# Splitting late weight loads into 256 KB pieces and shifting TensorE's instruction stream by six tiny products

## The chip, the cores and the metric

The kernel runs on one core of a Trainium2 chip. The metric is the device time of one execution in microseconds (us). Before the change the median of three timed executions is 273.48 us (272.48 to 273.54). A further execution was profiled: it took 271.83 us, and the stretch between its first and last instruction, the span on which all times below are counted, is 270.0 us.

The engines are called by the profile's names: PE (matrix products), DVE (vector work), ACT (activations and copies), POOL (GpSimd, which here copies blocks and issues most loads) and SP (which issues the stores). PEld is the loading of PE's stationary operand.

## What is computed

Block-sparse attention over 4 batches, 8 heads, 768 positions and head size 64, followed by a two-layer network on the 3072 resulting rows of 512 numbers. Cut to what matters:

```python
scores = scale * np.matmul(q, k.transpose(0, 1, 3, 2))
mask = (np.abs(blk_i - blk_j) <= 1) | (blk_i == 0) | (blk_j == 0) | (blk_i == 23) | (blk_j == 23)
for qb in range(24):                       # blocks of 32 positions
    for kb in sampled_blocks[qb]:          # three sampled blocks for each
        mask[qb*32:(qb+1)*32, kb*32:(kb+1)*32] = True
attn = softmax(np.where(mask, scores, -1e9))
x = (attn @ v).transpose(0, 2, 1, 3).reshape(3072, 512)
h = x @ w_in                               # 512 x 2048
out = (0.5 * h * (1 + erf(h / sqrt(2)))) @ w_out   # 2048 x 512
```

## The kernel before, in words

The work is cut into eight units, two for each batch. A unit is 384 rows of the output: three quads of 128. The first unit of a batch also holds the two blocks that see every key (its "dense" rounds). For a unit the kernel runs attention, then `ffn1_step` eight times (products with `w_in`, Gelu on ACT, result in `g`), and the second layer (`ffn2_pieces`, products of `g` with `w_out`, 16 for a quad, m = 0 to 15) is not run by itself: its products are the filler that is strewn among the next unit's attention.

The order of all instructions is written out by hand. `attention` takes a plan, a string of words, and each engine executes its own instructions in the order in which the words issue them: `s7` is the scores of round 7 (PE), `m7` the maxima (DVE), `e7` the exponentials (ACT), `t7` the transposition (DVE), `wb` the products with the values for group b (PE), `db` the division (DVE), `ob` the turning of the result (PE and ACT), `f4` four products from the filler, `xb` an extra step of that letter, `G` the load of the Gelu table on ACT. An upper-case `O` splits the copy in two. Unit 0 has no second layer before it, so its filler is `idle_products`: products whose result nobody reads.

Unit 0 has rounds 0 to 3 (dense), 4 and 5 (group a), 6 and 7 (group b), 8 and 9 (group c); round 9 has one block row instead of two, so 8 products instead of 16. In its plan `xa`, `xb`, `xc` begin the first layer ahead of its step (`ffn1_ahead`, whose triples are m, i and the number of columns done).

Loads go through POOL's queue, in the order of the program, between POOL's own copies. `w_in` is loaded in four column quarters (`load_w_in`, 0 to 3, needed by `ffn1_step` from m = 0, 4, 8 and 12), `w_out` in two halves (`load_w_out`, m = 0 to 7 and 8 to 15). Quarters 2 and 3 and both halves are issued in `values_of(0)` and `values_of(2)`, the words `xv0` and `xv2`, among POOL's 33 copies of sampled value blocks (into `kn` and `g`, used as spare room). Then `later_keys` (word `xl`) issues the keys and queries of batch 1: kn heads 0 to 3, qn heads 0 to 3, kn heads 4 to 7, qn heads 4 to 7. In `PLANS[1]`, the plan of unit 1, the words `xk0d`, `xk1`, `xq1d`, `xq0`, `xk2` and so on turn these, two heads at a time.

The matching lines of the profile: L361 scores, L486 and L447 products with values, L518 turning, L541 first layer, L584 second layer, L594 idle products, L241 turning of keys and queries, L161, L166 and L117 the loads of w_in, w_out and keys or queries.

Of the kernel before, what the change touches and what calls it, by code (L numbers as in the profile page):

```python
# [20 lines left out]
def kernel(  # L21
# [10 lines left out]
    nc = tc.nc  # L32
    P = 128
    B, H, S, D = q.shape
    assert (B, H, S, D) == (4, 8, 768, 64)
    BL = 32
# [8 lines left out]
    KC = NPR * BL  # L45
    BW = KC + 2 * VS
# [69 lines left out]
    def load_kq(dst, src, hs, b=0):  # L116
        nc.gpsimd.dma_start(out=dst[0:PP, hs],  # L117
                            in_=src[b, hs].rearrange("h (p i) d -> p h (i d)", i=PI))
# [36 lines left out]
        for h in VORDER[at]:  # L155
            load_v(b, h)

    def load_w_in(part, n=4):
        w = D_FF // n
        cols = slice(w * part, w * part + w)  # L160
        nc.gpsimd.dma_start(  # L161
            out=w_in_sb[:, :, cols], in_=moe_w_in[:, cols].rearrange("(ki p) f -> p ki f", p=P))

    def load_w_out(part, n=4):
        w = KOUT // n
        nc.gpsimd.dma_start(  # L166
            out=w_out_sb[:, w * part:w * part + w, :],
            in_=moe_w_out[P * w * part:P * w * (part + 1)].rearrange("(ko p) f -> p ko f", p=P))
# [141 lines left out]
    def gather(unit, js, at, c0=0, c1=BW, engine=None):  # L310

        src = k0 if (unit.b, c1) == (0, KC) else kvs[unit.b % 2][:, :, c0:c1]
        for j in js:
            for r in range(NR):
                to = sampled_values(unit, j, r) if c0 == KC else sampled(unit.place[j], r)[:, c0:c1]
                (engine or nc.vector).tensor_copy(to[:, None, :], src[:, bass.ds(at[j][r], 1), :])  # L316
# [270 lines left out]
                    finished.append((n, quad, slice(0, D_MODEL), op))  # L587
                yield

    def idle_products(m):  # L590

        op = psO.tile([P, D_MODEL], F32, name="op", tag="op")
        for _ in range(m):
            nc.tensor.matmul(op, lhsT=identity, rhs=qT0[:, 0:2, 0:2, :], start=True, stop=True)  # L594
            yield

    def store_finished():
# [109 lines left out]
    def values_of(t):  # L707

        def ask():
            js = grps[t]  # L710
            gather(units[0], js[:3], others, KC, BW, nc.gpsimd)
            if t != 1:
                load_w_in(2 + t // 2)
            gather(units[0], js[3:], others, KC, BW, nc.gpsimd)
            if t == 2:
                load_w_out(0, 2)
                load_w_out(1, 2)
        return ask

    def later_keys():  # L720
        for hs in HALVES:
            load_kq(kn, k, hs, 1)
            load_kq(qn, q, hs, 1)
        others.update(block_numbers(J1[8:], POOL))

    def more_numbers(js):
        def load():
            for c in range(0, len(js), 6):
                known.update(block_numbers(js[c:c + 6], DVE))
        return load  # L730
    attention(units[0], idle_products(32),
# [3 lines left out]
              {"l": later_keys, "p2": partial(later_pair, 0), "p3": partial(later_pair, 1),  # L735
               "h": lambda: fixed(0, None, 0, (0,)), "i": lambda: fixed(0, None, 0, (1, 2)),
               "j": lambda: fixed(0, None, 1),
# [1 line left out]
               "f2": lambda: fixed(2, nc.scalar.copy, 0), "v0": values_of(0), "v1": values_of(1),  # L739
               "v2": values_of(2), "n": more_numbers(J1[:3]),  # L740
               "a": lambda: ffn1_ahead(0, (0, 0, P), (0, 1, P)),
               "b": lambda: ffn1_ahead(0, (0, 0, 2 * P)),
               "c": lambda: ffn1_ahead(0, (0, 1, 2 * P), (2, 0, 2 * P), (2, 1, 2 * P))})

    def next_keys(b):
        place_keys(b)
        spare_key(keys(b))

    PLANS = {
# [109 lines left out]
```

## Time and profile before

| | |
|---|---|
| median of three timed executions | 273.48 us |
| profiled execution | 271.83 us |
| its span | 270.0 us |
| PE busy | 248.2 us (92%) |
| ACT busy | 205.6 us (76%) |
| DVE busy | 201.7 us (75%) |
| POOL busy | 103.8 us (38%) |
| span of unit 0's attention on PE (scores to the last turning) | 12.7 to 37.6 us |
| unit 0's first layer on PE, to its end | 37.4 to 49.5 us |
| unit 1's attention with unit 0's second layer | 49.5 to 71.9 us |

A timeline row of the profile reads: start and length in us, engine, line, operation, tile written <- tiles read, shape, count, and in brackets the idle time of the engine before it with what ended it. "issue" there means that the engine waited for nothing that the profile shows. In the page's part on DMA queues, q0 holds what POOL issues and q8 and q14 carry packets of the kind "instruction". In a row on DMA issues the last number is the median time from issue to landing.

### The profile page before, as it was taken

The page shows a single profiled execution, that of the slowest core. Times are in us where ns is not written, and L with a number is a line of the kernel's source. Part 1 is how long each engine was busy: PE and PEld are TensorE (multiplying, and loading weights), DVE is VectorE, ACT ScalarE, POOL GpSimd, SP SyncE. Part 2 cuts the span into 40 slices and gives each one's busy share as a digit, 9 for nine tenths or more (in the row PEclk, how much of TensorE's full clock was granted, in tenths as well). Part 3 has the DMA queues.
Part 4 walks back from the last instruction along what each step waited for, and adds up shares of the span by engine and source line. Part 5 has one row for each costly group of instructions (what it writes and reads, how often), then busy time and mean ns, then how long its engine had stood idle before and what let it go on. Part 6 is the DMA issues. An engine that isn't in the chain of part 4 may idle for free.

```text
span 270.0 us, 11525 instructions
## 1 busy us (share of the span) xinstructions
PE 248.2 (92%) x4909; PEld 143.6 (53%) x4944; DVE 201.7 (75%) x472; ACT 205.6 (76%) x379; POOL 103.8 (38%) x212
## 2 busy tenths in 40 slices
PE   0899688999999999999999999999999999999994
PEld 0634365455664665545555565455645655465544
DVE  7599768599998988599988987696979892981000
ACT  8789655987869867898779965987889676994611
POOL 7798970725974000943970004900040250000000
PEclk9999999999999999999999999999999999999999
DMA  6999489979999116922997019911101110111012
GB/s 96 187 187 143 70 130 200 206 138 137 93 169 154 41 44 133 129 17 87 140 158 130 22 64 140 99 41 45 39 4 41 44 41 0 41 44 41 0 39 83
DMA packets 75910, 24.41 MB, mean 90 GB/s; under 512 B 65489, under 2 KB 72914, under 8 KB 75858
## 3 DMA queue, kind: packets, MB, share of 16 engines
q0 software_dynamic: 57440, 13.64, 54.0%
q1 hardware_dynamic: 18418, 10.03, 14.5%
q8 instruction: 39, 0.64, 1.0%
q14 instruction: 13, 0.11, 0.1%
HBM read 27.26 MB, written 6.29 MB: 124 GB/s over the span
## 4 chain that ended last, share of the span: by engine, by line
PE 77%; ACT 9%; DVE 5%; issue 4%; DMA 3%; POOL 1%; POOLq 0%; ACTq 0%
PE hp L541 31%; PE op L584 23%; PE av L486 8%; PE sc L361 6%; ACT pp L404 3%; DMA qn<-in_q_dram 3%; ACT pp L408 2%; PE tx L518 2%; PE op L613 2%; PE pt L241 2%; PE av L447 2%; DVE pT L421 1%; DVE nm L387 1%; PE av L613 1%; DVE xh L506 1%
## 5 line engine op out<-in xcount | busy, mean ns | idle before, releaser
L541 PE MATMUL hp<-xT,w_in_sb 128*128 128x384 bf16 (+2 forms) x536 | 85.1, 319 | 1.3 <-issue 1.3
L584 PE MATMUL op<-w_out_sb,g 128*128 128x512 bf16 x302 | 75.5, 380 | 3.4 <-issue 2.3
L404 ACT ACTIVATE pp<-sc,nm 128x256 bf16<-128x256 f32 x176 | 73.8, 544 | 5.5 <-DVE nm L387 5.2
L541 PEld LDWEIGHTS <-w_in_sb 128*128 128x128 bf16 x536 | 51.2, 98 | 34.5 <-issue 1.5
L563 ACT ACTIVATE g<-hp 128x768 bf16<-128x768 f32 x56 | 45.1, 808 | 24.3 <-PE hp L541 24.2
L387 DVE TENSOR_REDUCE nm<-sc 128x4 f32<-128x1024 f32 (+1 forms) x48 | 52.9, 1115 | 13.9 <-PE sc L361 13.8
L584 PEld LDWEIGHTS <-g 128*128 128x128 bf16 x336 | 29.1, 98 | 34.1 <-issue 6.7
L316 DVE COPY gb<-kv 128x392 bf16 x177 | 35.4, 278 | 0.0
L421 DVE STREAM_TRANSPOSE pT<-pp 128x512 f32<-128x512 f32 (+1 forms) x48 | 30.5, 650 | 2.9 <-ACT pp L404 2.9
L172 POOL COPY mark<-gb 1x1 bf16<-1x1 bf16 x6 | 1.1, 179 | 80.7 <-DVE gb L316 80.7
L316 POOL COPY gb<-kv 128x392 bf16 x54 | 26.3, 537 | 13.7 <-PE av L486 13.4
L486 PEld LDWEIGHTS <-pT 64*32 64x32 bf16 (+1 forms) x2400 | 25.2, 91 | 8.1 <-issue 2.8
L486 PE MATMUL av<-kv,pT 64*32 64x130 bf16 (+1 forms) x1344 | 27.3, 221 | 1.6 <-issue 0.7
L526 ACT COPY xT<-tx 128x512 bf16<-128x512 bf16 (+3 forms) x32 | 13.6, 451 | 14.3 <-PE tx L518 14.3
L148 POOL DMA_DIRECT2D kv<-in_v_dram x32 | 22.9, 729 | 2.3 <-issue 2.2
L361 PE MATMUL sc<-gb,qT 64*32 64x256 bf16 x704 | 17.9, 274 | 2.8 <-issue 1.8
L432 ACT ACT_TABLE_LOAD x15 | 19.2, 1283 | 0.3
L361 PEld LDWEIGHTS <-qT 64*32 64x32 bf16 x832 | 9.8, 90 | 17.9 <-issue 9.8
L506 DVE TENSOR_TENSOR xh<-av,rec 128x512 bf16<-128x512 f32 (+2 forms) x28 | 18.2, 652 | 1.0
L390 DVE TENSOR_REDUCE nm<-sc 128x1 f32<-128x768 f32 x16 | 14.8, 946 | 4.2 <-PE sc L361 4.2
L408 ACT ACTIVATE pp<-sc,nm 128x768 bf16<-128x768 f32 x16 | 17.2, 1109 | 1.0 <-DVE nm L390 0.9
L568 ACT COPY os<-op 128x512 f32<-128x512 f32 (+1 forms) x23 | 13.2, 574 | 5.8 <-PE op L613 4.3
(81 smaller groups left out, 250.8 us busy)
## 6 DMA issues: line engine op xcount, KB each, us to landing
out_dram<-os SPq DMA_DIRECT2D x23, 256.0 KB, 2.1
kv<-in_v_dram POOLq DMA_DIRECT2D x32, 96.0 KB, 3.6
w_in_sb<-in_moe_w_in_dram POOLq DMA_DIRECT2D x4, 512.0 KB, 7.7
w_out_sb<-in_moe_w_out_dram POOLq DMA_DIRECT2D x2, 1024.0 KB, 13.3
kn<-in_k_dram POOLq DMA_DIRECT2D x4, 384.0 KB, 11.3
qn<-in_q_dram POOLq DMA_DIRECT2D x4, 384.0 KB, 12.6
qn<-in_q_dram POOLq DMA_DIRECT2D x12, 128.0 KB, 5.3
kn<-in_k_dram POOLq DMA_DIRECT2D x12, 128.0 KB, 5.4
```

The source lines that it names most:

```text
L148: nc.gpsimd.dma_start(out=kvs[b % 2][32 * hh:32 * hh + 32, 0:NB, c0:c0 + D], in_=v[b, h].rearrange("(n p) d -> p n d", p=BL))
L316: (engine or nc.vector).tensor_copy(to[:, None, :], src[:, bass.ds(at[j][r], 1), :])
L361: nc.tensor.matmul(o, lhsT=qT[rows, j // 4, pr, BL * (j % 4):BL * (j % 4) + BL], rhs=rhs(rows, pr), start=True, stop=True)
L387: nc.vector.tensor_reduce(out=nm[:, 0:2 * n].rearrange("p (g j) -> p g j", g=2), in_=A4[:, :, 0:n, :], op=ALU.max, axis=AX.X, negate=True)
L404: nc.scalar.activation(at[:, x // n, x % n], A[:, a:a + 256].rearrange("p (e c k) -> p e c k", e=2, k=BL), AF.Exp, bias=nm[:, x:x + 1])
L408: nc.scalar.activation(pp[:, 0:S].rearrange("p (c k e) -> p c e k", e=2, k=BL), A[:, 0:S].rearrange("p (c e k) -> p c e k", e=2, k=BL), AF ...
L421: nc.vector.transpose(pt.rearrange("p g c x -> p (g c) x")[:, :, 64 * s:64 * (s + n)].bitcast(F32), pp[:, 0:512 * n].bitcast(F32).rearrang ...
L486: nc.tensor.matmul(av[32 * s:32 * (s + w), h, VS * G:VS * G + V2], lhsT=pv[rows, G, c % 4, BL * s:BL * (s + w), c // 4], rhs=src[rows], st ...
L506: nc.vector.tensor_tensor(xh[rows, :, 0:m * D].rearrange("p h (g x d) -> p h g x d", x=2, d=D), a[:, :, :, 0:2 * D].rearrange("p h g (x d) ...
L541: nc.tensor.matmul(hp[:, i, c0:c1], lhsT=w_in_sb[:, ki, (m + i) * P:(m + i + 1) * P], rhs=xTs[n % 2][:, ki, c0:c1], start=(ki == 0), stop= ...
L563: nc.scalar.activation(g[:, m:m + 2, 0:T], hp[:, :, 0:T], AF.Gelu)
L584: nc.tensor.matmul(op, lhsT=g[:, m, t * P:(t + 1) * P], rhs=w_out_sb[:, m, :], start=(m == 0), stop=(m == KOUT - 1))
```

## The change

Four things change; no arithmetic of the result does.

1. Loads. `load_w_in` gets a number of pieces, and quarter 3 comes in two pieces along the rows (256 KB each). `w_out` comes in eight pieces of two m each (256 KB each) instead of two halves. Pieces 0 to 5 stand where the halves stood; pieces 6 and 7 are issued in `later_keys` behind the first load of keys.
2. Quarter 2 of `w_in` (the third) is issued behind all twelve copies of its group instead of behind nine.
3. `idle_products` gets a set of places at which the product has 32 x 32 outputs instead of 128 x 512. There are six of these, and they come ahead of the six full ones before `s7`, the eighth scores of unit 0. Four full idle products are added ahead of `wb`, and two are taken out behind `Oc`.
4. `ffn1_ahead` no longer does columns 128 to 256 of m = 0 ahead (8 products of 128 columns); `ffn1_step` then does columns 128 to 384 in 8 products of 256 columns instead of 8 of 128. In `PLANS[1]` one second-layer product moves from before `xk0d` to behind it.

```diff
-    def load_w_in(part, n=4):
+    def load_w_in(part, n=4, pieces=1):
         w = D_FF // n
         cols = slice(w * part, w * part + w)
-        nc.gpsimd.dma_start(
-            out=w_in_sb[:, :, cols], in_=moe_w_in[:, cols].rearrange("(ki p) f -> p ki f", p=P))
+        for ki in range(0, KIN, KIN // pieces):
+            rows = slice(ki, ki + KIN // pieces)
+            nc.gpsimd.dma_start(
+                out=w_in_sb[:, rows, cols],
+                in_=moe_w_in[P * rows.start:P * rows.stop, cols].rearrange("(ki p) f -> p ki f", p=P))
...
-    def idle_products(m):
+    def idle_products(m, small):
         op = psO.tile([P, D_MODEL], F32, name="op", tag="op")
-        for _ in range(m):
-            nc.tensor.matmul(op, lhsT=identity, rhs=qT0[:, 0:2, 0:2, :], start=True, stop=True)
+        for n in range(m + len(small)):
+            if n in small:
+                nc.tensor.matmul(op[0:BL, 0:BL], lhsT=identity[:, 0:BL], rhs=qT0[:, 0, 0, 0:BL], start=True, stop=True)
+            else:
+                nc.tensor.matmul(op, lhsT=identity, rhs=qT0[:, 0:2, 0:2, :], start=True, stop=True)
             yield
...
-            gather(units[0], js[:3], others, KC, BW, nc.gpsimd)
+            gather(units[0], js, others, KC, BW, nc.gpsimd)
             if t != 1:
-                load_w_in(2 + t // 2)
-            gather(units[0], js[3:], others, KC, BW, nc.gpsimd)
+                load_w_in(2 + t // 2, pieces=1 + t // 2)
             if t == 2:
-                load_w_out(0, 2)
-                load_w_out(1, 2)
+                for part in range(6):
+                    load_w_out(part, 8)
...
             load_kq(kn, k, hs, 1)
+            if hs is HALVES[0]:
+                load_w_out(6, 8)
+                load_w_out(7, 8)
             load_kq(qn, q, hs, 1)
...
-    attention(units[0], idle_products(32),
+    attention(units[0], idle_products(34, range(16, 22)),
...
-              "e4 t3 t2 s5 f1 xf2 wd0 s6 f1 xv2 wd1 f2 m5 f2 e5 t4 m6 f2 dd s7 t5 e6 m7 od f2 s8 t6 wa xl e7 f4 "
-              "m8 s9 da e8 m9 t7 t8 e9 t9 f2 oa wb wc db ob dc xn xa Oc xb f2 G xc",
+              "e4 t3 t2 s5 f1 xf2 wd0 s6 f1 xv2 wd1 f8 m5 f2 e5 t4 m6 f2 dd s7 t5 e6 m7 od f2 s8 t6 wa xl e7 f4 "
+              "m8 s9 da e8 m9 t7 t8 e9 t9 f2 oa f4 wb wc db ob dc xn xa Oc G xb",
...
-               "b": lambda: ffn1_ahead(0, (0, 0, 2 * P)),
-               "c": lambda: ffn1_ahead(0, (0, 1, 2 * P), (2, 0, 2 * P), (2, 1, 2 * P))})
+               "b": lambda: ffn1_ahead(0, (2, 0, 2 * P), (2, 1, 2 * P))})
...
-        1: ("S s0 s1 m0 m1 f8 e0 f5 xk0d t0 f3 e1 s2 f3 xk1 m2 S t1 s3 e2 f3 m3 f2 xq1d xv t2 wa da e3  "
+        1: ("S s0 s1 m0 m1 f8 e0 f4 xk0d t0 f4 e1 s2 f3 xk1 m2 S t1 s3 e2 f3 m3 f2 xq1d xv t2 wa da e3  "
```

Three places show what moves. The first is POOL's queue at the end of unit 0's value copies (`g<-kv`), ahead of the copies for unit 1. Before:

```order
L316 COPY g<-kv_83 128x264
L161 DMA w_in_sb<-in_moe_w_in_dram 128x4x512
L166 DMA w_out_sb<-in_moe_w_out_dram 128x8x512 x2
L117 DMA kn<-in_k_dram 96x4x512
L117 DMA qn<-in_q_dram 96x4x512
L117 DMA kn<-in_k_dram 96x4x512
L117 DMA qn<-in_q_dram 96x4x512
L230 TENSOR_LOAD vf
L172 COPY mark<-gb 1x1
```

The same place with the change (L163 is `load_w_in`, L169 `load_w_out`):

```order
L319 COPY g<-kv_83 128x264
L163 DMA w_in_sb<-in_moe_w_in_dram 128x2x512 x2
L169 DMA w_out_sb<-in_moe_w_out_dram 128x2x512 x6
L117 DMA kn<-in_k_dram 96x4x512
L169 DMA w_out_sb<-in_moe_w_out_dram 128x2x512 x2
L117 DMA qn<-in_q_dram 96x4x512
L117 DMA kn<-in_k_dram 96x4x512
L117 DMA qn<-in_q_dram 96x4x512
L233 TENSOR_LOAD vf
L175 COPY mark<-gb 1x1
```

Seven loads became fourteen of the same bytes in all, and the first keys now stand ahead of the last quarter of w_out.

The second place is PE around `s7` and `s8` of unit 0: the turning of group d (`tx`), two idle products (`op`), and the first product of `s8` (`sc`), which is row 694 of PE's program. Before:

```order
L361 LDWEIGHTS qT_86
L361 MATMUL sc<-gb,qT_86 32x256
L518 LDWEIGHTS xh
L518 MATMUL tx<-identity,xh 128x128
L518 LDWEIGHTS xh
L518 MATMUL tx<-identity,xh 128x128
L594 LDWEIGHTS identity
L594 MATMUL op<-qT_86,identity 128x512
L594 LDWEIGHTS identity
L594 MATMUL op<-qT_86,identity 128x512
L361 LDWEIGHTS qT_86
L361 MATMUL sc<-gb,qT_86 32x256
```

With the change, the six tiny products stand behind the dense group's products with the values and ahead of the full idle ones (here the last two tiny and the first two full ones, rows 649 to 656):

```order
L598 LDWEIGHTS identity
L598 MATMUL op<-qT_86,identity 32x32
L598 LDWEIGHTS identity
L598 MATMUL op<-qT_86,identity 32x32
L600 LDWEIGHTS identity
L600 MATMUL op<-qT_86,identity 128x512
L600 LDWEIGHTS identity
L600 MATMUL op<-qT_86,identity 128x512
```

From there on PE's instructions stand 12 rows later: row 694 is now the fifteenth product of `s7`, and the first product of `s8` is row 706.

The third place is PE at `s9`. Before, its eight products are rows 941 to 956, behind idle products; rows 937 to 944:

```order
L594 LDWEIGHTS identity
L594 MATMUL op<-qT_86,identity 128x512
L594 LDWEIGHTS identity
L594 MATMUL op<-qT_86,identity 128x512
L361 LDWEIGHTS qT_86
L361 MATMUL sc<-gb,qT_86 32x256
L361 LDWEIGHTS qT_86
L361 MATMUL sc<-gb,qT_86 32x256
```

With the change, rows 943 to 954 hold the last product of `wa`, the four idle products and the first product of `s9`:

```order
L489 LDWEIGHTS pT
L489 MATMUL av<-kv_83,pT 128x130
L600 LDWEIGHTS identity
L600 MATMUL op<-qT_86,identity 128x512
L600 LDWEIGHTS identity
L600 MATMUL op<-qT_86,identity 128x512
L600 LDWEIGHTS identity
L600 MATMUL op<-qT_86,identity 128x512
L600 LDWEIGHTS identity
L600 MATMUL op<-qT_86,identity 128x512
L364 LDWEIGHTS qT_86
L364 MATMUL sc<-gb,qT_86 32x256
```

So row 949, the fifth product of `s9` before, now belongs to the third of the idle products ahead of it.

Both programs have 9890 rows on PE; behind the second layer's products around `xk0d` (row 1680) they have the same instruction in the same row again.

## The prediction

> **What bounds the kernel now.** I read the page first, then what PE waited for, then PE's timeline through unit 0, then the DMA queues stretch by stretch.
>
> ```profile
> span 270.0 us, 11525 instructions
> q8 instruction: 39, 0.64, 1.0%
> PE 77%; ACT 9%; DVE 5%; issue 4%; DMA 3%; POOL 1%; POOLq 0%; ACTq 0%
> ```
>
> PE carries the end (77% of the chain). The change touches only the first 55 us, so what counts is where PE stands idle there. The list of PE's waits has, behind the wait for the first keys, mostly "issue":
>
> ```profile
> PE sc L361 <- issue: 2.0, 2, 1.8
> PE hp L541 <- issue: 1.3, 1, 1.3
> PE av L486 <- issue: 0.7, 2, 0.4
> ```
>
> PE's timeline places them:
>
> ```profile
> 25.41 0.41 PE L361 MATMUL sc<-gb,qT 64*32 64x256 bf16 x16
> 26.91 0.41 PE L361 MATMUL sc<-gb,qT 64*32 64x256 bf16 x16 [0.43 <-ACT pp L404]
> 28.43 1.04 PE L594 MATMUL op<-qT,identity 128*128 128x512 bf16 x4
> 29.40 0.29 PE L361 MATMUL sc<-gb,qT 64*32 64x256 bf16 x4
> 31.48 0.29 PE L361 MATMUL sc<-gb,qT 64*32 64x256 bf16 x4 [1.79 <-issue]
> 33.19 0.70 PE L486 MATMUL av<-kv,pT 64*128 64x130 bf16 x32 [0.66 <-DVE pT L421]
> 35.03 0.29 PE L486 MATMUL av<-kv,pT 64*32 64x130 bf16 x9 [0.37 <-issue]
> 41.50 8.02 PE L541 MATMUL hp<-xT,w_in_sb 128*128 128x128 bf16 x49 [1.35 <-issue]
> ```
>
> Three holes, A (1.79 us, in the middle of `s9`), B (0.37, in `wc`) and C (1.35, in the first layer), 3.51 us in all. None stands where a wait is written. By PE's order `s9` stops ahead of row 949, and counting products from there B and C stop near rows 1205 and 1461: 256 rows apart. The page has 39 packets of kind "instruction" on q8 for PE's 9890 rows, 254 rows each, 0.64 MB (the row has packets, MB and share) / 39 = 16 KB. I read the holes as PE having run out of program. The DMA view shows one such packet before each hole's end:
>
> ```profile
> q0 software_dynamic: 423, 0.43, 119.3%
> ...
> q8 instruction: 1, 0.02, 5.5%
> ...
> q8 instruction: 1, 0.02, 5.3%
> ...
> q0 software_dynamic: 619, 0.62, 106.3%
> ...
> q8 instruction: 1, 0.02, 5.5%
> ```
>
> The first is 26.9 to 29.1 us (only POOL's loads, no q8), the second 29.1 to 30.2 (the packet for row 949), the third 32.6 to 33.9 (for row 1205; nothing else moves), the fourth 35.0 to 39.1 (loads alone) and the last 39.1 to 40.2 (for row 1461). PE goes on at 31.48, 35.03 and 41.50 us, 1.1 to 1.3 us behind these stretches' ends. The packet seems to be asked for when PE steps over the boundary before: row 693 at 26.91 (the load of `s8`'s first operand, held by ACT), row 949 at 31.48, row 1205 at 35.03. Crossing to packet start is then 2.2, 1.1 and 4.1 us. The 1.1 has an empty DMA queue; in the other two POOL's `w_in` and `w_out` loads are moving. So a packet waits behind loads, by 1.1 us at A and 3.0 us at C.
>
> [...]
>
> **The change part by part.**
>
> *Six tiny products and the later quarter (hole A).* The chain of waits has the nearest prices:
>
> ```profile
> 28.50 0.97 PE op L594 x4
> ...
> 37.22 0.34 PE tx L518 x4
> ...
> 63.19 1.27 PE av L486 x104
> ```
>
> In size the tiny products lie between an `av` product (0.012 us) and a turning (0.085 us): 0.07 to 0.5 us for six. I take 0.2, since `s8` waits for ACT until 26.91 and `s7` ends at 25.8: 0.43 us of idle time covers it. What they do is put row 693 into `s7`, so that PE crosses at about 26.0 and not at 26.91; with those 1.1 us the packet reaches the queue at 27.1. The third quarter's place:
>
> ```profile
> 24.38 0.74 POOL L161 DMA_DIRECT2D w_in_sb<-in_moe_w_in_dram  x1
> 25.11 1.10 POOL L316 COPY kn<-kv 128x264 bf16 x3
> 33.49 0.74 POOL L161 DMA_DIRECT2D w_in_sb<-in_moe_w_in_dram  x1
> 34.22 1.77 POOL L166 DMA_DIRECT2D w_out_sb<-in_moe_w_out_dram  x2
> 35.96 0.71 POOL L117 DMA_DIRECT2D kn<-in_k_dram  x1
> ```
>
> It moves behind the three copies: issued at 25.4, it fills the queue from about 27.6 instead of 26.5. The packet then gets in ahead (0.5 us to spare), takes 1.0, and PE has its rows at 27.1 + 1.0 + 1.3 = 29.4. PE reaches row 949, now the third idle product ahead of `s9`, at 28.9: hole A shrinks to 0.5. If the packet loses that race, it starts at 30.2 and hole A grows by 1 us; that is its other bound. With 29.4, `s9` is done at 30.1 instead of 31.8. DVE waits for it (1.92 us in the row below), so `m9` starts at 30.15:
>
> ```profile
> 31.82 0.69 DVE L387 TENSOR_REDUCE nm<-sc 128x2 f32<-128x512 f32 x1 [1.92 <-PE sc L361]
> ```
>
> *Four more idle products ahead of `wb`* (1.0 us, the 0.97 above). `t7` would free `wb` at 31.5; with two idle products, the turning and these four PE comes there at 31.8. They replace the 0.66 us wait and cost 0.3. `wb` gains 33.19 - 31.8 = 1.4 us.
>
> *Hole B.* Row 949 crossed at 29.4, packet in the queue at 30.5, third quarter still moving until about 31.3: PE has it between 32.9 and 33.6 and needs it at 33.1. Between 0 and 0.5 us remains; I take 0.2, gain 0.2.
>
> *Hole C, two idle products fewer, 8 products merged.* Row 1205 is crossed at 33.3, so its packet arrives at 34.4, ahead of the first byte of the last quarter (issued at 33.49, moving from 35.0): usable at 36.8, needed at about 38 (PE came to it at 40.15, less 1.6 from `wb` and B and 0.4 from the next edit). Hole C goes (gain 1.3; if the packet comes late it waits for a 256 KB piece and not 512 KB, and 0.5 remains). The two idle products give 0.43. Merging 8 products of 128 columns into 256-column ones leaves the columns as they are: nothing. Sum for PE at the start of unit 1: 1.4 + 0.2 + 1.3 + 0.4 = 3.3 us, first scores at 46.3 to 46.6 instead of 49.45 (DVE's copies for them end at 48.1 and move with the 1.5 us of `wc`: 46.6).
>
> *The loads, which take most of it back.* PE comes 3 us earlier to work that needs w_out and the keys, and these do not come earlier. POOL's queue still gets to the last quarter at 33.49, since its copies wait for none of this. Landings:
>
> ```profile
> w_in_sb<-in_moe_w_in_dram POOLq DMA_DIRECT2D x1, 512.0 KB, 5.3
> DMA to landing us min/median/max: 11.0/13.3/15.6
> kn<-in_k_dram POOLq DMA_DIRECT2D x1, 384.0 KB, 16.6
> qn<-in_q_dram POOLq DMA_DIRECT2D x1, 384.0 KB, 17.8
> kn<-in_k_dram POOLq DMA_DIRECT2D x1, 384.0 KB, 19.1
> qn<-in_q_dram POOLq DMA_DIRECT2D x1, 384.0 KB, 20.7
> ```
>
> The rows are the last quarter (33.49 + 5.3 = 38.8), the two halves of w_out (34.22 + 11.0 = 45.2; 35.10 + 15.6 = 50.7), and the keys and queries, issued from 35.96 on: 52.6, 54.4, 56.4, 58.7. From 38.8 to 52.6 us 2048 + 384 KB land, 5.7 us per 1000 KB. With the change, piece 5 (m = 10, 11) lands at 38.8 + 1536 x 0.0057 = 47.5, the first keys at 49.7, piece 6 at 51.1 and piece 7 (m = 14, 15) at 52.6, as the keys did before: the same bytes stand ahead of it. Issue is no limit: ten pieces at about 0.7 us each hold POOL for 4.5 us more than 0.74 + 1.77, until 43 to 45 us, and its next work waits for DVE until 48.19, then 46.6.
>
> PE before:
>
> ```profile
> 50.01 2.98 PE L584 MATMUL op<-w_out_sb,g 128*128 128x512 bf16 x12
> 52.92 0.53 PE L241 MATMUL pt<-identity,kn 96*64 96x96 bf16 x16
> 53.38 0.82 PE L584 MATMUL op<-w_out_sb,g 128*128 128x512 bf16 x3
> 54.13 0.41 PE L361 MATMUL sc<-gb,qT 64*32 64x256 bf16 x16
> ```
>
> With the change: two scores to 47.1, 12 products (m = 0 to 11) at 0.25 to 50.0, keys turned to 50.6, m = 12 and 13 at 51.2 to 51.7, then PE waits for piece 7 until 52.6, does m = 14 and 15 (0.5) and starts `s2` at 53.1 instead of 54.13: 1.0 us gained. One instruction packet instead of two falls into this run of loads, which ends the slowest of the 16 engines' share 0.3 to 0.5 us earlier; gain 1.0 to 1.5, taken as 1.2. So of 3.3 us PE wins, some 2 stand again as a wait for w_out. This also makes the result insensitive to A, B and C: 2 of the 3.3 us may fail.
>
> *After 54 us.* PE's program is row for row the same, and the queries (54.4) and later keys (56.4, 58.7) are used from 57.23 and 60.99 on: 1.2 us earlier still fits. The packet asked for behind `s2` again meets 384 KB loads, between no wait and a whole load's 1.9 us, against about 1.0 now: -0.3 (a hole of 0.29 at 59 us goes) to +1; I take 0. Later loads are started by the computation and move with it.
>
> **Sum** against the profiled execution: 271.83 - 1.2 = 270.6 us. It lies 1.65 below the median of the runs shown, so the forecast for that is 273.48 - 1.2 = 272.3.
>
> **The rivals.** (1) *The loads come in sooner too.* The later loads land 384 KB in 1.9 us (5.0 us per 1000 KB). At that pace piece 7 lands at 38.8 + 12.2 = 51.0, `s2` starts at 51.5 and 2.6 us are won: 270.9. Against it: the first half of w_out took 6.4 us for 1024 KB beside the same first layer.
>
> (2) *It does not do what it says.* The packet loses the race at A, its successors queue behind small loads as behind large ones, PE is at `s0` when it was before, and only the order of loads differs: 273.3, no change. For it: margins of 0.5 us; against it: C has 1.2 us, and 1.0 of gain needs only that.
>
> (3) *Slower: each load costs something of its own.* Ahead of `m = 15` stand 10 loads where 4 stood ahead of the keys' turning. If each boundary costs as much as the landings of the small loads differ (1.9 to 2.3 us, so 0.4), the six more cost 2.4 us, `s2` starts at 55.5, and the time is 274.7. From 0.2 us each it decides. Against it: 384 KB loads land at 200 KB per us, 1024 KB ones (45.2 to 50.7) at 186.
>
> [...]
>
> **How the numbers follow.** Forecast 0.57, rival 1 0.15, rival 2 0.19, rival 3 0.09. What tells from no change is 0.5%, 1.4 us, so faster means under 272.1: nearly half of the forecast (0.57 x 0.47 = 0.27), rival 1 (0.15) and a little of rival 2: 0.44. Slower than 274.85 has half of rival 3, and late packets behind `s2` together with rival 2: 0.10. Within: 0.46. The range takes in rivals 1 and 2 and some of the jitter of later packets, 270.4 to 274.0; the forecast's own is 271.6 to 273.0.
>
> **What would show it.** Right: no hole inside `s9`; the first layer without the 1.35 us; unit 1's first scores near 46.5; then PE waiting 1 to 2 us for w_out ahead of `s2`, which starts near 53. Wrong: a hole of over 1 us still at rows 949 or 1461; no wait for w_out at all (rival 1); piece 7 landing after 54 (rival 3); or a clock below full after the wait for w_out.

## The result, and the profile after

The change makes the kernel slower by half a percent: 273.65 us (median of 22, 272.37 to 275.48) against 272.63 us for the kernel before (22 executions beside it), a ratio of 1.0051 (95% interval 1.0033 to 1.0068). The ratio is formed from the undisturbed executions and not from the two medians, whose quotient is 1.0037. The forecast was 1.2 us faster; the 273.48 us that it started from is the median of three of these 22 executions of the kernel before. The profiled execution after has a span of 271.4 us against 270.0.

The chain of waits and the list of PE's waits, after:

```profile
span 271.4 us, 11567 instructions
PE 86%; ACT 4%; DMA 3%; issue 2%; DVE 2%; POOL 1%; POOLq 0%; ACTq 0%
```

```profile
PE op L600 <- issue: 2.6, 1, 2.6
PE hp L544 <- issue: 1.5, 1, 1.5
PE sc L364 <- issue: 0.4, 1, 0.4
```

PE's holes with no written wait add up to 4.5 us where they were 3.5. PE's timeline places them (L600 is a full idle product, L364 scores, L489 values, L544 first layer):

```profile
25.78 0.41 PE L364 MATMUL sc<-gb,qT 64*32 64x256 bf16 x15
26.57 0.28 PE L364 MATMUL sc<-gb,qT 64*32 64x256 bf16 x1 [0.38 <-issue]
...
28.95 0.60 PE L600 MATMUL op<-qT,identity 128*128 128x512 bf16 x2
32.15 1.03 PE L600 MATMUL op<-qT,identity 128*128 128x512 bf16 x2 [2.59 <-issue]
33.12 0.41 PE L364 MATMUL sc<-gb,qT 64*32 64x256 bf16 x8
33.46 1.04 PE L600 MATMUL op<-qT,identity 128*128 128x512 bf16 x2
34.29 0.63 PE L521 MATMUL tx<-identity,xh 128*128 128x128 bf16 x4
34.72 1.33 PE L600 MATMUL op<-qT,identity 128*128 128x512 bf16 x4
35.98 0.70 PE L489 MATMUL av<-kv,pT 64*128 64x130 bf16 x32
...
43.62 8.02 PE L544 MATMUL hp<-xT,w_in_sb 128*128 128x128 bf16 x49 [1.53 <-issue]
51.57 0.63 PE L364 MATMUL sc<-gb,qT 64*32 64x256 bf16 x32
...
56.26 0.41 PE L364 MATMUL sc<-gb,qT 64*32 64x256 bf16 x16
```

Read against the rows before: there is a new hole of 0.38 us ahead of the last product of `s7`, where row 693 now stands. Hole A, at row 949, grew from 1.79 to 2.59 us and ends at 32.15 instead of 31.48. It used to lie in the middle of `s9`; now all of `s9` and eight idle products come behind it and ahead of `wb`. `wb` starts at 35.98 instead of 33.19, 2.8 us later. Hole B is gone (0.37 us back) and two idle products are fewer (0.43). Hole C is still there, 1.53 instead of 1.35. `s2` of unit 1 starts at 56.26 instead of 54.13. Of these 2.1 us some 0.9 come back behind `s2`: the kernel before has four more small holes there (0.16, 0.29, 0.16 and 0.25 us between 56 and 66 us), and the changed kernel has none.

DMA view after, for 26.6 to 29.9, 29.9 to 31.0, 37.4 to 41.3 and 41.3 to 42.4 us:

```profile
q0 software_dynamic: 514, 0.52, 103.9%
...
q8 instruction: 1, 0.02, 5.5%
...
q0 software_dynamic: 665, 0.64, 105.9%
...
q8 instruction: 1, 0.02, 5.5%
```

The first stretch moves 514 of POOL's packets and no instruction packet. That is the third quarter of w_in (a quarter is 128 x 4 rows, 512 packets) all but its last few. The packet for row 949 starts only behind it, near 29.9 us, where it started near 29.1 before. The packet for row 1461 starts near 41.3 us, 4.2 us behind PE's crossing of row 1205 in the fourth product of `wc` (37.1), although the loads in the queue are now 256 KB each.

Then the clock. The engines' busy time in stretches, after (start, end, length, then PE, PEld, DVE, ACT and POOL with their counts, then granted clock, share of the DMA engines and GB/s):

```profile
26.00:30.00 4.00, 3.18 (x142) 1.78 (x127) 3.25 (x6) 3.21 (x10) 4.00 (x12) 1.00 0.88 135
30.00:32.20 2.20, 0.05 (x1) 0.06 (x2) 0.84 (x2) 1.65 (x4) 2.20 (x7) 0.93 0.00 0
32.20:36.00 3.80, 3.80 (x22) 1.33 (x24) 2.23 (x4) 1.37 (x3) 3.80 (x8) 0.59 0.32 45
36.00:40.00 4.00, 3.43 (x215) 3.01 (x215) 2.21 (x7) 0.60 (x2) 3.76 (x7) 1.00 1.01 147
```

Behind the hole of 2.59 us the granted clock is 0.59 of full over 32.2 to 36.0 us. The idle products, `s9` and a turning run in it: two full idle products take 1.03 us, where four took 1.04 before. From the hole's end to `wb` PE needs 3.83 us (32.15 to 35.98).

### The profile page after: what moved, and what is told of

Same layout as the page of the kernel before. It is cut to its first block, busy times and chain, and to the rows that moved or that the text cites. A ratio compares the mean times of both kernels' runs of the same rounds, so it can differ in the third digit from the quotient of the medians.

```text
span 271.4 us, 11567 instructions
## 1 busy us (share of the span) xinstructions
PE 254.5 (94%) x4944; PEld 144.2 (53%) x4944; DVE 202.2 (75%) x472; ACT 205.7 (76%) x379; POOL 108.5 (40%) x219
## 3 DMA queue, kind: packets, MB, share of 16 engines
HBM read 27.26 MB, written 6.29 MB: 124 GB/s over the span
## 4 chain that ended last, share of the span: by engine, by line
PE 86%; ACT 4%; DMA 3%; issue 2%; DVE 2%; POOL 1%; POOLq 0%; ACTq 0%
PE hp L544 31%; PE op L587 25%; PE av L489 9%; PE sc L364 7%; PE op L600 4%; DMA qn<-in_q_dram 3%; PE tx L521 2%; PE av L450 2%; PE op L619 2%; PE pt L244 2%; PE av L619 1%; ACT pp L407 1%; ACT L435 1%; ACT pp L411 1%; DVE pT L424 1%
## 5 line engine op out<-in xcount | busy, mean ns | idle before, releaser
L544 PE MATMUL hp<-xT,w_in_sb 128*128 128x384 bf16 (+2 forms) x528 | 84.9, 321 | 1.5 <-issue 1.5
L587 PE MATMUL op<-w_out_sb,g 128*128 128x512 bf16 x336 | 83.4, 380 | 0.0
L544 PEld LDWEIGHTS <-w_in_sb 128*128 128x128 bf16 x528 | 51.0, 98 | 34.5 <-issue 1.7
L587 PEld LDWEIGHTS <-g 128*128 128x128 bf16 x336 | 29.1, 98 | 33.4 <-issue 6.0
L319 POOL COPY gb<-kv 128x392 bf16 x54 | 26.3, 539 | 13.6 <-PE av L489 13.3
L489 PEld LDWEIGHTS <-pT 64*32 64x32 bf16 (+1 forms) x2400 | 25.2, 91 | 6.8 <-issue 1.9
L489 PE MATMUL av<-kv,pT 64*32 64x130 bf16 (+1 forms) x1344 | 26.9, 221 | 0.0
L364 PEld LDWEIGHTS <-qT 64*32 64x32 bf16 x832 | 9.8, 90 | 16.5 <-issue 9.3
L364 PE MATMUL sc<-gb,qT 64*32 64x256 bf16 x704 | 18.0, 275 | 0.6 <-issue 0.4
```

The source lines that it names most:

```text
L364: nc.tensor.matmul(o, lhsT=qT[rows, j // 4, pr, BL * (j % 4):BL * (j % 4) + BL], rhs=rhs(rows, pr), start=True, stop=True)
L489: nc.tensor.matmul(av[32 * s:32 * (s + w), h, VS * G:VS * G + V2], lhsT=pv[rows, G, c % 4, BL * s:BL * (s + w), c // 4], rhs=src[rows], st ...
L544: nc.tensor.matmul(hp[:, i, c0:c1], lhsT=w_in_sb[:, ki, (m + i) * P:(m + i + 1) * P], rhs=xTs[n % 2][:, ki, c0:c1], start=(ki == 0), stop= ...
L587: nc.tensor.matmul(op, lhsT=g[:, m, t * P:(t + 1) * P], rhs=w_out_sb[:, m, :], start=(m == 0), stop=(m == KOUT - 1))
```

## The experiments

Four theories, in the words used in the expectations. S: the tiny products shift the program, and the new boundary in the eighth scores makes the loss. L: the small loads do. I: the four idle products ahead of `wb` do. Q, formed after the first four runs: the later third quarter alone does, because the packet for row 949 has to let it pass. W is about the hole in the first layer. Ratios are to the kernel before, each with its 95% interval.

**x1, the six tiny products late.**

```diff
-    attention(units[0], idle_products(34, range(16, 22)),
+    attention(units[0], idle_products(34, range(28, 34)),
-              "... xv2 wd1 f8 m5 ... m8 s9 da e8 ..."
+              "... xv2 wd1 f2 m5 ... m8 s9 f6 da e8 ..."
```

> The changed kernel with the six tiny products moved from ahead of the eighth scores to behind the tenth scores, so that the boundaries at rows 693 and 949 lie where they lay before the change, and all rows behind are those of the changed kernel. Theory S (the shifted program: the boundary in the eighth scores makes a new hole of 0.4 us, and the hole at row 949 then holds back all of the tenth scores and four idle products): no hole in the eighth scores, the hole at row 949 is again inside the tenth scores and shorter than 2.59 us, ratio to before 0.998 to 1.002. Theory L (the small loads are slow or collide) and theory I (the four idle products ahead of the values of group b cost 1 us): ratio stays 1.004 to 1.007.

Measured: 1.0046 (1.0014 to 1.0078). The hole in `s7` is gone and the one at row 949 is back inside `s9`, but it is 2.93 us:

```profile
27.12 0.41 PE L364 MATMUL sc<-gb,qT 64*32 64x256 bf16 x16 [0.43 <-ACT pp L407]
32.84 0.37 PE L364 MATMUL sc<-gb,qT 64*32 64x256 bf16 x4 [2.93 <-issue]
```

S fails: without the shift nearly all of the loss is still there.

**x2, the third quarter back behind nine copies.**

```diff
-            gather(units[0], js, others, KC, BW, nc.gpsimd)
-            if t != 1:
-                load_w_in(2 + t // 2, pieces=1 + t // 2)
+            gather(units[0], js[:3], others, KC, BW, nc.gpsimd)
+            if t == 0:
+                load_w_in(2)
+            gather(units[0], js[3:], others, KC, BW, nc.gpsimd)
+            if t == 2:
+                load_w_in(3, pieces=2)
```

> The changed kernel with the third quarter of w_in again behind nine copies instead of twelve. Theory S with the later quarter as a part of it (the packet for row 949 waits for that quarter to pass): the packet starts about 1 us earlier, near 29.1 us, the hole at row 949 is about 1.6 us, ratio 1.000 to 1.003. Theories L and I: ratio 1.004 to 1.007.

Measured: 1.0014 (0.9986 to 1.0042). By the middle values most of the loss is gone with this edit alone; the intervals overlap. Its holes, and `wb`:

```profile
27.33 0.28 PE L364 MATMUL sc<-gb,qT 64*32 64x256 bf16 x1 [0.95 <-issue]
31.26 0.60 PE L600 MATMUL op<-qT,identity 128*128 128x512 bf16 x2 [0.95 <-issue]
33.66 0.70 PE L489 MATMUL av<-kv,pT 64*128 64x130 bf16 x32
...
41.76 8.02 PE L544 MATMUL hp<-xT,w_in_sb 128*128 128x128 bf16 x49 [1.71 <-issue]
```

PE leaves hole A at 31.26, near the 31.48 of the kernel before, and the clock stays full. From there to `wb` it needs 2.40 us for the instructions that took 3.83 in the changed kernel. What A loses the hole at row 693 takes (0.95): the packet for that row started late in this execution (24.7 us, 24.1 in the changed kernel) and PE stood there longer.

**x3, the loads whole again** (w_in's last quarter in one piece, w_out in two halves, all keys and queries behind them; the rest as changed).

```diff
-                load_w_in(2 + t // 2, pieces=1 + t // 2)
+                load_w_in(2 + t // 2)
-                for part in range(6):
-                    load_w_out(part, 8)
+                load_w_out(0, 2)
+                load_w_out(1, 2)
-            if hs is HALVES[0]:
-                load_w_out(6, 8)
-                load_w_out(7, 8)
```

> The changed kernel with the loads of w_in's last quarter and of w_out whole and in the order of before. Theory L: the 1 us comes back, ratio 0.999 to 1.001, and the packet behind row 1205's crossing starts later than with small loads. Theory S and I: ratio 1.004 to 1.007; and if small loads shorten no packet's wait, crossing to packet start near 38 us stays about 4 us as with them.

Measured: 1.0048 (1.0021 to 1.0074). L fails. The packet for row 1461 does not wait longer behind small loads either. DMA view for 36.4 to 40.8 and 40.8 to 41.9 us:

```profile
q0 software_dynamic: 799, 0.80, 118.9%
...
q8 instruction: 1, 0.02, 5.5%
```

PE crossed row 1205 at 36.38 (its hole B ends there), so the packet started 4.4 us behind. With 256 KB loads it was 4.2, before the change 4.1.

**x4, the four idle products away from `wb`.**

```diff
-              "... t9 f2 oa f4 wb wc db ob dc xn xa Oc G xb"
+              "... t9 f2 oa wb wc db ob dc xn xa Oc f4 G xb"
```

> The changed kernel with the four idle products moved from ahead of the values of group b to behind the last turning of unit 0. Theory I: 1 us comes back, ratio 1.000 to 1.002. Theory S: they cost at most the part that does not lie beside the wait for the transposition, some 0.5 us, ratio 1.002 to 1.005. Theory L: 1.004 to 1.007.

Measured: 1.0036 (1.0010 to 1.0062). I is not the main part: 0.0036 of the 0.0051 is left by the middle values, and the intervals overlap.

Only the place of the third quarter had clearly moved the time, so the next four runs move it alone.

**y1, the kernel before with the quarter behind twelve copies.**

```diff
-            gather(units[0], js[:3], others, KC, BW, nc.gpsimd)
+            gather(units[0], js, others, KC, BW, nc.gpsimd)
             if t != 1:
                 load_w_in(2 + t // 2)
-            gather(units[0], js[3:], others, KC, BW, nc.gpsimd)
```

> The kernel before with one edit: the third quarter of w_in behind all twelve copies instead of nine. Theory Q (the later quarter alone makes the loss: the packet for row 949 now has to let the whole quarter pass): packet starts near 30 us instead of 29.1, hole at row 949 about 2.6 us, ratio to before 1.003 to 1.007. Theory S (the tiny products shift the boundary, and that makes the loss): ratio 0.998 to 1.002.

Measured: 1.0030 (1.0004 to 1.0056). By the middle values this one edit brings three fifths of the loss into the kernel before; the interval reaches from almost none of it to all. Timeline, and stretches from 30.0 us:

```profile
32.52 0.29 PE L361 MATMUL sc<-gb,qT 64*32 64x256 bf16 x4 [2.51 <-issue]
```

```profile
30.00:32.50 2.50, 0.01 (x4) 0.00 (x0) 0.23 (x1) 0.99 (x3) 2.50 (x9) 1.00 0.13 23
32.50:37.00 4.50, 3.82 (x174) 3.07 (x178) 2.81 (x7) 1.37 (x3) 4.50 (x9) 0.62 0.46 60
```

Hole A is 2.51 us where it was 1.79, and the clock behind it is 0.62, without tiny products, small loads or more idle products.

**y2, the kernel before with the quarter ahead of the twelve copies.**

```diff
-            gather(units[0], js[:3], others, KC, BW, nc.gpsimd)
-            if t != 1:
-                load_w_in(2 + t // 2)
-            gather(units[0], js[3:], others, KC, BW, nc.gpsimd)
+            if t == 0:
+                load_w_in(2)
+            gather(units[0], js, others, KC, BW, nc.gpsimd)
+            if t == 2:
+                load_w_in(3)
```

> The kernel before with the third quarter of w_in ahead of the twelve copies, where POOL waits anyway. Theory Q: the quarter has passed by 28 us, the packet for row 949 starts at 28.0 to 28.4 us, the hole there falls from 1.8 to 0.7 to 1.0 us, ratio 0.995 to 0.999. Theory S: the place of the quarter matters little, ratio 0.999 to 1.001.

Measured: 0.9975 (0.9949 to 1.0001). Hole A falls to 0.94, as expected, but two other things take it back:

```profile
27.70 0.41 PE L361 MATMUL sc<-gb,qT 64*32 64x256 bf16 x16 [1.11 <-POOL g L316]
31.43 0.29 PE L361 MATMUL sc<-gb,qT 64*32 64x256 bf16 x4 [0.94 <-issue]
...
42.27 8.02 PE L541 MATMUL hp<-xT,w_in_sb 128*128 128x128 bf16 x49 [2.17 <-issue]
```

`s8` starts 0.8 us later than before, and the wait ahead of it is put down to POOL; hole C is 2.17 us in this execution. The last quarter and w_out are issued 0.7 us earlier there and stand ahead of C's packet, which fits, but was not tried by itself.

**y3, the changed kernel with the quarter ahead of the copies.**

```diff
-            gather(units[0], js, others, KC, BW, nc.gpsimd)
-            if t != 1:
-                load_w_in(2 + t // 2, pieces=1 + t // 2)
+            if t == 0:
+                load_w_in(2)
+            gather(units[0], js, others, KC, BW, nc.gpsimd)
+            if t == 2:
+                load_w_in(3, pieces=2)
```

> The changed kernel with the third quarter of w_in ahead of the twelve copies. Theory Q: the packet for row 949 starts at 27.6 to 28.0 us and the hole there is at most 0.7 us; PE reaches unit 1 some 1 to 2 us earlier than in the kernel before, and the last piece of w_out near 52.6 us sets the rest; ratio 0.993 to 0.998. Theory S: the new boundary in the eighth scores and the idle products still cost, ratio 1.001 to 1.005.

Measured: 1.0002 (0.9972 to 1.0031). The loss is gone, but the gain that Q expected (0.993 to 0.998) is not there. Hole A is 0.94 us, but the hole in `s7` is 1.47 us, 0.38 in the changed kernel. That the quarter now delays the packet for row 693 fits this, but was not shown.

```profile
27.41 0.28 PE L364 MATMUL sc<-gb,qT 64*32 64x256 bf16 x1 [1.47 <-issue]
31.34 0.60 PE L600 MATMUL op<-qT,identity 128*128 128x512 bf16 x2 [0.94 <-issue]
...
42.39 9.70 PE L544 MATMUL hp<-xT,w_in_sb 128*128 128x128 bf16 x49 [1.99 <-issue]
```

**y4, the changed kernel with the quarter later still**, behind six of the copies into `g`.

```diff
-            gather(units[0], js, others, KC, BW, nc.gpsimd)
-            if t != 1:
-                load_w_in(2 + t // 2, pieces=1 + t // 2)
+            gather(units[0], js[:2], others, KC, BW, nc.gpsimd)
+            if t == 1:
+                load_w_in(2)
+            gather(units[0], js[2:], others, KC, BW, nc.gpsimd)
+            if t == 2:
+                load_w_in(3, pieces=2)
```

> The changed kernel with the third quarter of w_in still later, behind six of the copies into g, so that the packet for row 949 (asked for near 26.5 us, at the queue near 27.7) goes ahead of it. Theory Q as a race: hole at row 949 at most 0.7 us, ratio 0.993 to 0.999; the packet for row 1205 may now wait for the quarter, with a hole of up to 1 us in the values of group c. If later is simply worse: hole of 2.6 us or more, ratio 1.005 to 1.010.

Measured: 0.9997 (0.9967 to 1.0027), again without the gain. Later is not worse in itself: in the changed kernel nine copies ahead of the quarter give 1.0014, twelve 1.0051 and eighteen 0.9997. The packet now goes ahead of the quarter, hole A is 0.67 us and PE leaves it at 30.53:

```profile
26.87 0.28 PE L364 MATMUL sc<-gb,qT 64*32 64x256 bf16 x1 [0.61 <-issue]
30.53 0.60 PE L600 MATMUL op<-qT,identity 128*128 128x512 bf16 x2 [0.67 <-issue]
...
40.90 8.02 PE L544 MATMUL hp<-xT,w_in_sb 128*128 128x128 bf16 x49 [1.44 <-issue]
```

**z1, the kernel before with the weights held.** A copy on POOL that waits for the last copy of unit 0's result stands ahead of w_in's last quarter, w_out and the keys and queries (the edit is cut to what adds it).

```diff
+    def held_weights():
+        xT, t0 = column[0, 3]
+        hold_loads(xT[0:1, 0, t0:t0 + 1])
+        load_w_in(3)
+        load_w_out(0, 2)
+        load_w_out(1, 2)
+        later_keys()
-              "... wa xl e7 ... Oc xb f2 G xc"
+              "... wa e7 ... Oc xl xb f2 G xc"
```

> The kernel before, with all loads behind POOL's value copies (the last quarter of w_in, both halves of w_out, keys and queries) held until the last turning of unit 0 is copied out, near 38 us, so that nothing is in the queue when PE crosses row 1205 near 35 us. If waiting behind loads makes the hole in the first layer (theory W): the packet starts 1.1 to 1.3 us behind the crossing, near 36.2 us, and the hole of 1.35 us is gone; w_out then lands 4 to 5 us late and the time as a whole grows to 276 to 279 us. If the hole is something else (a fixed delay): the packet again starts 4.1 us behind the crossing and the hole stays over 1 us.

Measured, on two executions only: 1.0144 (1.0077 to 1.0210), 276.05 us, as W has it. DMA view for 36.1 to 37.2 us, then PE's waits:

```profile
DMA packets 1, 0.02 MB, mean 15 GB/s; under 512 B 0, under 2 KB 0, under 8 KB 0
q8 instruction: 1, 0.02, 7.1%
```

```profile
34.98 0.29 PE L486 MATMUL av<-kv,pT 64*32 64x130 bf16 x9 [0.38 <-issue]
...
54.50 1.94 PE L584 MATMUL op<-w_out_sb,g 128*128 128x512 bf16 x5 [3.19 <-DMA w_out_sb<-in_moe_w_out_dram]
```

The packet starts 1.1 us behind the crossing at 34.98, alone in the queue, and there is no hole in the first layer any more. So the loads in the queue make hole C. The price is the wait for w_out (0.90 us ahead of this row and the 3.19), and a half clock over 54.9 to 58.3 us behind it.

**z2, y4 with the tiny products late** (the edit against y4).

```diff
-    attention(units[0], idle_products(34, range(16, 22)),
+    attention(units[0], idle_products(34, range(28, 34)),
-              "... xv2 wd1 f8 m5 ... m8 s9 da e8 ..."
+              "... xv2 wd1 f2 m5 ... m8 s9 f6 da e8 ..."
```

> The changed kernel with the third quarter behind six of the copies into g, as in y4, and the six tiny products behind the tenth scores. Theory S (the boundary in the eighth scores brings row 949's packet earlier, at the price of a hole of 0.4 to 0.6 us in the eighth scores): packet for row 949 near 28.5 to 29 us instead of 28.2, or behind the quarter near 31, ratio 1.000 to 1.004. If the tiny products bring nothing: ratio 0.998 to 1.000, as y4.

Measured: 0.9990 (0.9966 to 1.0013), against 0.9997 for y4 in the batch before: the tiny products bring nothing that can be measured. PE's holes in `s9` and the first layer, and a wait for the weights:

```profile
30.77 0.29 PE L364 MATMUL sc<-gb,qT 64*32 64x256 bf16 x4 [0.95 <-issue]
...
40.39 8.02 PE L544 MATMUL hp<-xT,w_in_sb 128*128 128x128 bf16 x49 [0.89 <-issue]
52.95 0.59 PE L587 MATMUL op<-w_out_sb,g 128*128 128x512 bf16 x2 [0.29 <-DMA w_out_sb<-in_moe_w_out_dram]
```

**z3, y4 with `wb` free** (the edit against y4).

```diff
-              "... t9 f2 oa f4 wb wc db ob dc xn xa Oc G xb"
+              "... t9 f2 oa wb wc db ob dc xn xa Oc f4 G xb"
```

> The changed kernel with the third quarter behind six of the copies into g, as in y4, and the four idle products behind the last turning of unit 0 instead of ahead of the values of group b. Theory I (they hold the values back): 0.3 to 1.0 us earlier than y4, ratio 0.996 to 0.999. If the transposition releases the values anyway: as y4, 0.999 to 1.001.

Measured: 0.9991 (0.9966 to 1.0017). No difference to y4 in the time that can be told. In the trace the four idle products hold `wb` back by 0.12 us: from hole A's end PE needs 2.28 us to `wb` here and in x4, and 2.40 in x2, y3 and y4.

**z4, the kernel before with the quarter behind twelve copies and six into `g`** (y4's order of copies and loads, with the loads whole).

```diff
-            gather(units[0], js[:3], others, KC, BW, nc.gpsimd)
-            if t != 1:
-                load_w_in(2 + t // 2)
-            gather(units[0], js[3:], others, KC, BW, nc.gpsimd)
+            gather(units[0], js[:2], others, KC, BW, nc.gpsimd)
+            if t == 1:
+                load_w_in(2)
+            gather(units[0], js[2:], others, KC, BW, nc.gpsimd)
             if t == 2:
+                load_w_in(3)
                 load_w_out(0, 2)
```

> The kernel before with one edit: the third quarter of w_in behind the twelve copies and six of those into g. Theory Q as a race: the packet for row 949 (crossing at 26.9 us) starts near 28.1 us ahead of the quarter, hole there 0.7 to 1.0 us, ratio 0.996 to 0.999. If later is worse in itself: ratio 1.004 to 1.008.

Measured: 0.9977 (0.9951 to 1.0003). There is no hole at row 949 in this execution; B and C are 1.32 and 0.80 us.

```profile
34.64 0.29 PE L486 MATMUL av<-kv,pT 64*32 64x130 bf16 x9 [1.32 <-issue]
40.57 8.02 PE L541 MATMUL hp<-xT,w_in_sb 128*128 128x128 bf16 x49 [0.80 <-issue]
```

z4 and y2 are the best of the versions run, a quarter of a percent below the kernel before with intervals that end at 1.000. They beat the changed kernel, and whether they beat the one before these runs do not settle.

Taken together, all five versions with the third quarter behind twelve copies (the changed kernel, x1, x3, x4, y1) lie between 1.0030 and 1.0051, with intervals above 1. The seven with it elsewhere and the weights not held lie between 0.9975 and 1.0014, with intervals that take in 1.

## Why the prediction was wrong, point by point

*What bounds PE there* was right: the holes with no written wait lie 256 rows apart, PE goes on 1.1 to 1.3 us behind a stretch with one instruction packet (in the changed kernel too: the stretches end at 31.0 and 42.4, PE goes on at 32.15 and 43.62), and loads in the queue lengthen the holes. z1 shows it with the queue empty (start 1.1 us behind the crossing, hole C gone), y1 with a load moved by three copies (hole A 1.79 to 2.51). That PE is out of program there is a reading of these packets; no row of the profile says it.

*The six tiny products and the later quarter* is the step that failed, and it failed on the margin. The prediction let PE cross row 693 "at about 26.0" and gave the packet "0.5 us to spare" ahead of the quarter. But the rows behind 693 come in a packet themselves. The trace before already had it, from 24.1 to 25.0 us (DMA view for 24.0 to 25.1):

```profile
q8 instruction: 1, 0.02, 5.4%
```

With the 1.1 to 1.3 us that PE took behind such a stretch at A, B and C, it would have crossed at 26.1 to 26.3 at the earliest, by estimate. In the changed kernel the packet ran from 24.1 to 25.3 and PE had the rows only at 26.57 (the 0.38 us hole in `s7`), so moving the boundary forward bought 0.3 us and not 0.9. With 1.1 us more (31.48 to 32.6 for row 1205's packet before, in an empty queue) the packet for row 949 would have been at the queue near 27.7, again an estimate. The quarter's first packets moved there from 26.6, and from 27.6, as forecast, it filled the queue. So the margin was gone, and the packet started near 29.9 us, behind nearly all 512 packets of the quarter. The other bound, a start at 30.2 with hole A 1 us longer, was written down, and nearly that happened (0.8 us longer). Which half of this pair cost the time is told apart by x1 and y1: without the shift and with the later quarter it is 1.0046, with the later quarter alone 1.0030 (y1), and with the shift but the quarter back 1.0014 (x2). The quarter is the larger part; what is left over is within these intervals.

*The price of losing the race* was mis-sized. I had the extra 1 us of hole A fall into the slack ahead of the weights, and rival 2 therefore ended at no change. Two things were left out. Hole A no longer splits `s9` but comes ahead of all of it and of eight idle products, so nothing of these was done when PE stopped. And the clock: the 2.59 us of idle PE ran into 3.4 us at half clock (granted 0.50 over 31.91 to 35.32 us), in which those very products ran.

`wb` started 2.8 us later, and the traces give the parts. The hole ends 0.67 us later. From its end to `wb` PE needs 1.71 us in the order of before (31.48 to 33.19, and the same in y1) and 2.40 in the new order at full clock (x2, y3, y4; x3 the same within 0.01): 0.69. At half clock it needed 3.83: 1.43 more. So in the profiled execution the clock is the largest part. The new order alone does not make the loss: x1 and y1 have hole A inside `s9`, as before the change, and still lose nearly all of it (x1) and three fifths (y1).

The clocks of the other executions fit this. A mean granted clock of 0.994 or less, which one such stretch of half clock gives (0.993 in the changed kernel's profile), stands in 63 of the 69 executions of the five versions with the quarter behind twelve copies, in 38 of 97 of the kernel before (those beside x1 to z4), and in 13 of 83 of the seven others. The 63 took 273.6 us in the mean, and the six at full clock 272.7, where the kernel before took 272.2 at full clock. No run changes the clock alone, and with six executions these shares are rough.

*The four idle products* were costed at 0.3 us. The times of x4 and z3 give no clear answer on a few tenths; their traces show 0.12 us at full clock.

*Hole C* was to vanish, and "waits for a 256 KB piece and not 512 KB" was the reason for its other bound. Both fell. PE crossed row 1205 at 37.1 and not at 33.3, too late to get the packet ahead of the loads. Even y4's crossing at 34.71 was too late: 1.1 us later, at 35.8, the loads had the queue full (its DMA engines are at full share from 35.2). The packet started 4.2 us behind the crossing with 256 KB pieces, 4.4 with whole loads (x3) and 4.1 before. The hole stayed, at 1.53.

*The loads* were right in time. The rows after for pieces 5, 6 and 7 (issued at 38.15, 39.84 and 41.34, time to landing last):

```profile
w_out_sb<-in_moe_w_out_dram POOLq DMA_DIRECT2D x1, 256.0 KB, 9.9
...
w_out_sb<-in_moe_w_out_dram POOLq DMA_DIRECT2D x1, 256.0 KB, 11.4
w_out_sb<-in_moe_w_out_dram POOLq DMA_DIRECT2D x1, 256.0 KB, 11.3
```

Pieces 5, 6 and 7 land at 48.0, 51.2 and 52.6 (47.5, 51.1 and 52.6 were forecast). So rival 3 falls: the additional loads cost nothing that shows in the time (x3, with whole loads, 1.0048). But "Issue is no limit" was too light: POOL waited 0.24, 0.79 and 1.63 us for earlier loads to land, ahead of pieces 6 and 7 and of the first queries, and issued the last queries at 45.75 instead of 37.97. In the changed kernel PE came too late to wait for w_out. In z2, where it came early, it did wait for piece 7, until 52.95, as the prediction's limit says. The gain that rival 1 and the forecast counted on is not there for another reason: where hole A shrinks, the others stay. y4's four holes (0.61, 0.67, 0.41 and 1.44 us, the third in `wc`) add up to 3.1 us against 3.5 before. With loads in the queue no version's trace has unit 1's first scores ahead of 48.34 (z2), where 46.5 was forecast and 49.45 was before. Rival 2, the packet that loses the race, is the one that came true, with a price that it did not have.

So the sign was wrong because the forecast rested on a race with 0.5 us of margin, and the margin on a crossing that PE could not reach in time. The size was wrong because a longer hole was priced by its length alone, without the work held up behind it and without the clock.

## What to carry to other kernels

When PE stands still with no wait written, look for instruction packets in the DMA queues and lay them beside the loads. Here a 512 KB load issued 0.8 us later made such a packet start 0.8 us later (29.1 to 29.9 us), and the same load issued later still let the packet go ahead (28.2 us in y4). Before moving a boundary in the program forward, check the packet with the rows behind it: here it ended only at 25.3 us, and PE was over the boundary 0.3 us earlier where 0.9 was forecast. When a hole grows, look at the clock behind it too (here 0.59 over the 3.8 us behind 2.59 us). Whether filler work is better placed ahead of a hole's end than behind it these runs do not show.

## What the runs showed that was not expected

- Holes of two us or more on PE were mostly followed by about 3.4 us at half clock: after 2.59 us in the changed kernel (clock 0.59 over the 3.8 us behind), after 2.51 in y1 (0.62 over 4.5 us), after 1.99 at C in y3 and x3 (49 products in 9.70 us where they take 8.02). It stayed full behind 1.79 in the kernel before, 2.17 in y2 and 2.59 at A in x3. So the length alone does not tell these cases apart.
- The place of a hole may matter. In the traces' clock records a half clock in the middle of the kernel lasts 3.41 us, and it comes 13.65 us (the changed kernel, at 31.91), 17.07 (x1, x4, y1), 27.31 (x3, y3) or 37.55 us (z1) behind the start of full clock: 4, 5, 8 and 11 times 3.41. In the 3.41 us ahead of it PE was busy for 1.06 us in the changed kernel, 0.48 in x1, 0.94 in y1, 1.60 in x4, 1.43 in x3, 1.42 in y3 and 0.40 in z1. Where the clock stayed full, the emptiest such stretches had 1.76 us in the kernel before, 1.70 in x2 and 1.51 in y2. The sum of work in such a stretch sorts the cases better than the hole's length, except for x4 and y2. No run was made to test it.
- The wait of an instruction packet behind loads did not follow their size: from crossing row 1205 to the packet's start it took 3.3 to 4.5 us with pieces of 256 KB (z2, y3) and 3.7 to 4.9 with loads of 512 KB and 1 MB (z4, y2), against 1.1 us with nothing in the queue.
- In z4 a packet started sooner behind the crossing than 1.1 us: the one for row 949 at 27.8, 0.55 us behind the first product of `s8` (27.26), and PE did not stop at all. When exactly it is asked for these runs do not say.
- Each hole is read from one profiled execution. Hole A of the kernel before is 1.79 us, and 1.55 in z1, whose program is the same up to there; in the changed order it is 2.59 in x3 and 2.87 in x4. So a difference of 0.3 us between two single holes can be chance.
